# Filling TensorE's first waits with identity products, writing its order by hand, and pulling the next batch's memory and first softmax into that order

## The chip, the cores and the metric

The kernel runs on one core of a Trainium2 chip. The metric is the device time of one execution in microseconds (us). A NeuronCore has a matrix engine (TensorE, PE in the profile, with PEld for its weight loads), a vector engine (VectorE, DVE), a scalar engine (ScalarE, ACT), GpSimd (POOL), and SyncE (SP), which here issues most of the transfers. Each engine runs its own list of instructions in order and waits on semaphores for the others.

## The reference

The program is an attention with a compressed memory, followed by two wide feed-forward layers. All arrays are float32.

```python
# q, k, v: [4, 8, 576, 64]; phi: [4, 8, 576, 32]
a = exp(phi - max(phi, axis=2)); a = a / (sum(a, axis=2) + 1e-09)   # over the sequence
k_m = einsum('bhsm,bhsd->bhmd', a, k); v_m = einsum('bhsm,bhsd->bhmd', a, v)
scores = (1 / sqrt(64)) * q @ k_m.T                                  # 32 memory slots
attn = softmax(scores); x = attn @ v_m                               # [2304, 512] over heads
h = maximum(x @ w_in1, 0); y = (h * h) @ w_out1                      # 512 -> 2048 -> 512
h = y @ w_in2; out = (h * tanh(softplus(h))) @ w_out2                # 512 -> 2048 -> 512
```

The weights reach the kernel as 64-bit floats and are turned into float32 on the chip.

## The kernel before

**Stages.** For each batch, `phi` is exponentiated along the sequence (`kv_soft`, L415 on), transposed on TensorE (`kv_turn`, tiles `pt` and `et`), and multiplied with k and v (`kv_mem`, tile `pk`); `kv_heads` turns the result into `kT` and `vT`. One batch has two halves of 288 tokens. `attn_unit` makes one half's scores (tile `psc`, L511) and runs their softmax in steps: two transposes, a maximum and a subtraction on VectorE (tile `x`), an exponential on ScalarE, then sum, reciprocal and product on VectorE, a transpose back (`at`), and a split into a high part (`ah`, ScalarE) and a low part (`al`, VectorE). v's memory is multiplied into the first weight matrix beforehand (`w_part`, tiles `pw` and `wp`), so that a half's hidden columns are six products of `ah` and `al` with `wp` (`h_products`, L655 to L657). ScalarE takes relu, square and high part (`s`, `g`), VectorE the low part of `g`, and twelve products L622 to L624 add one hidden chunk of 128 columns into four accumulators (`mm2_step`).

**Weights.** A slab of 512 KB of raw words (`raw_i` for w_in1, `raw_o` for w_out1, named i0, i1, o0 and so on below) is loaded by SyncE. ScalarE prepares it with one instruction ("pre"), VectorE joins the words with two ("first", L230, and "second", L236); a slab of w_out1 then gets a high part on ScalarE (`o1h`, L219) and a low part on VectorE (`o1l`, L279).

**What sets the order.** The helper `written(engine)` ties the instructions that are traced inside it to the order of the code, on the engines named. Around `first_memory()` and `first_tile()` it holds for VectorE and ScalarE: all of the first half's work (hidden chunks 0 to 3 of batch 0, half 0), the softmax of half 1, and the weight slabs they need stand in an order written by hand. TensorE's own order there is left to a scheduler, with a table `ahead` that puts four hidden products behind chosen products of the next batch's memory. The next batch's memory and its first softmax are made after that (`lanes = kv_later(1) + attn_later(1, 0)` in the loop over `subs`). TensorE starts with eight products of the identity with itself (`warm`, L714).

**Transfers.** SyncE has eight completion semaphores, so a transfer is issued only after the eighth before it has landed; the first 61 us of loads land one behind the other.

Of the kernel before, what the change touches and what calls it, by code (L numbers as in the profile page):

```python
# [18 lines left out]
P = 128  # L19
# [19 lines left out]
def body(tc, q, kvm, kvt, phi, w_in1, w_out1, w_in2, w_out2, out):  # L39
    nc = tc.nc  # L40
# [37 lines left out]
    def load_phi(b, p):  # L78
        nc.sync.dma_start(phi_t[p][:, at[p]:at[p] + S], phi[b, p])
# [14 lines left out]
    def load_q(b, half):  # L94

        q_t[b, half] = []
        for i in range(2):
            if b < 2 and half == 1:
                t = wo.tile([P, 2, T], F32, tag=f"wo{'hl'[i]}4", name=f"q{b}{half}{i}")
            else:  # L100
                t = Y.tile([P, 2, T], F32, tag="q", name=f"q{b}{half}{i}", bufs=2)
            nc.sync.dma_start(
                t.rearrange("p g t -> p (g t)"), q[b, half, :, 2 * i * T:2 * (i + 1) * T])
            q_t[b, half].append(t)
# [9 lines left out]
    def load_first(i):  # L114
        for p in range(2):
            nc.sync.dma_start(kv_t[0, p][i].rearrange("p g c d -> p (g c d)"), kvm[0, p, i])
        nc.sync.dma_start(tails[:, i].rearrange("p g d -> p (g d)"), kvt[0, i])

    load_first(0)
    load_q(0, 0)  # L120
# [285 lines left out]
    def banks2(name):  # L406
# [2 lines left out]
    rc_t, et_t, kk_t, kT, vT = {}, {}, {}, {}, {}  # L409

    done_pe = {}
    ahead = {(0, 1, 0): ("pt", 1, 0), (0, 1, 1): ("pk", 1, 0), (0, 1, 2): ("pk", 1, 1),
             (0, 1, 3): ("psc", 1, 0)}

    def kv_soft(b, p):  # L415

# [57 lines left out]
    def kv_heads(b, which, tag):  # L474

        ps = bank(tag, f"pkt{b}{which[0]}")
        for i in which:
            done_pe["pkt", b] = nc.tensor.transpose(
                ps[:, i * P:i * P + P], kk_t[b, "k"][:, i].rearrange("p a d -> p (a d)"), ident)
        if 0 in which:  # L480
            kT[b] = Y.tile([P, P], F32, tag="kT", name=f"kT{b}", bufs=2)
            if which == (0,):
                nc.vector.tensor_scalar_mul(kT[b], ps[:, :P], 0.125)
            else:
                nc.scalar.mul(kT[b], ps[:, :P], 0.125)
        if 1 in which:
            vT[b] = Y.tile([P, P], F32, tag="vT", name=f"vT{b}", bufs=2)
            (nc.scalar.copy if which == (1,) else nc.vector.tensor_copy)(vT[b], ps[:, P:2 * P])

    def kv_unit(b, tag, nxt):  # L490
        for p in range(2):
# [214 lines left out]
    c1.hold = True  # L706
    c1.load(1)
    load_first(1)
    c1.load(4)
    load_q(0, 1)  # L710
    c1.load(3)
    warm = bank("acc3", "warm")
    for _ in range(N_WARM):
        nc.tensor.matmul(warm[:, :P], ident, ident, start=True, stop=True)  # L714


    def first_memory():
# [8 lines left out]
    def next_loads():  # L726
        load_phi(1, 0)
        load_phi(1, 1)
        load_kv(1, 0)
        load_tail(1)  # L730
        kv_t[1, 1] = tuple(page([P, 4, NC, D], F32, f"kv11{i}") for i in "kv")
        for i in range(2):
            nc.sync.dma_start(kv_t[1, 1][i].rearrange("p g c d -> p (g c d)"), kvm[1, 1, i])
        c1.load(1)
        load_q(1, 0)

    def first_tile():


        conv = c1.turn  # L740
        at00, at01 = (attn_unit(0, half, nxt, True) for half, nxt in (
            (0, None), (1, lambda: load_q(1, 1))))
        out_of, g, s = [], {}, {}

        def h(fc):
            s[fc] = h_products(0, 0, fc, ("mm", "b0")), X.tile([P, T], F32, tag="s", name=f"s00_{fc}", bufs=3)
            g[fc] = X.tile([P, 2, T], F32R, tag="g", name=f"g00_{fc}", bufs=4)

        def relu(fc):
            marks["step"] = nc.scalar.activation(s[fc][1], s[fc][0], AF.Relu)  # L750

        def square(fc):
            nc.scalar.activation(s[fc][1], s[fc][1], AF.Square)

        def high(fc):
            nc.scalar.copy(g[fc][:, 0], s[fc][1])

        def low(fc):
            marks["lo"] = nc.vector.tensor_sub(g[fc][:, 1], s[fc][1], g[fc][:, 0].bitcast(F32))

        def mm2(fc):
            pend.append((mm2_step, (
                out_of[0], fc, fc == 0, fc == GROUPS[0] - 1, g[fc][:, 0], g[fc][:, 1], out_of[1])))

        next(at00)
        next(at00)
        conv("pre", "i1", 0)
        next(at00)
        conv("first", "i1", 0)
        conv("second", "i1", 0)  # L770
        kv_mem(0, 0, (1,), "acc3")
        kv_mem(0, 1, (1,), "acc0")
        kv_heads(0, (1,), "acc1")
        with written(mybir.EngineType.SP):
            next_loads()
        conv("pre", "i1", 1)
        next(at00)
        next(at00)
        w_low = w_part(0, 0, 0, P, True)
        next(at00)  # L780
        w_low()
        conv("first", "i1", 1)
        conv("pre", "o1", 0)
        next(at00)
        conv("second", "i1", 1)
        out_of += acc_of(0, 0, 0, GROUPS[0])
        h(0)
        conv("first", "o1", 0)
        conv("pre", "i1", 2)
        relu(0)  # L790
        w_low = w_part(0, 0, P, 2 * P, True)
        conv("second", "o1", 0)
        with written(mybir.EngineType.SP):
            c1.load(3)
        conv("high", "o1", 0)
        square(0)
        high(0)
        w_low()
        h(1)
        conv("first", "i1", 2)  # L800
        conv("low", "o1", 0)
        low(0)
        mm2(0)
        run_pend(0)
        conv("pre", "i1", 3)
        conv("second", "i1", 2)
        relu(1)
        square(1)
        conv("first", "i1", 3)
        conv("second", "i1", 3)  # L810
        high(1)
        conv("pre", "o1", 1)
        low(1)
        w_low = w_part(0, 1, 0, 256, True)
        conv("first", "o1", 1)
        conv("second", "o1", 1)
        conv("high", "o1", 1)
        w_low()
        conv("low", "o1", 1)
        next(at01)  # L820
        h(2)
        h(3)
        mm2(1)
        run_pend(0)
        relu(2)
        square(2)
        high(2)
        next(at01)
        relu(3)
        square(3)  # L830
        next(at01)
        low(2)
        mm2(2)
        high(3)
        conv("pre", "o1", 2)
        conv("pre", "o1", 3)
        kv_soft(1, 0)
        next(at01)
        next(at01)
        next(at01)  # L840
        kv_soft(1, 1)
        next(at01)
        conv("first", "o1", 2)
        conv("second", "o1", 2)
        conv("high", "o1", 2)
        low(3)
        mm2(3)
        conv("first", "o1", 3)
        conv("low", "o1", 2)
        conv("second", "o1", 3)  # L850
        marks["step"] = conv("high", "o1", 3)
        conv("low", "o1", 3)

    def lazy(f):
        yield from f()
# [55 lines left out]
    for i, (f0, f1, b, half) in enumerate(subs):  # L911
        final = i == len(subs) - 1
        if i == 0:
# [3 lines left out]
            c1.hold = False  # L917
            c1.store()
            c1.load(2 * GROUPS[0] - 3)
            lanes = kv_later(1) + attn_later(1, 0)  # L920
            run_step(lanes, 7)
            continue
        elif i == 1:
            assert (0, 1) in a_t
# [446 lines left out]
```

## Time and profile before

| | us |
|---|---|
| median of 3 runs (lowest, highest) | 771.23 (769.04, 771.65) |
| the profiled execution | 770.25 |
| its span, first to last instruction | 768.3 |
| PE busy | 735.0 |
| DVE busy | 530.5 |
| ACT busy | 425.4 |

The profiled execution takes 1.95 us more than its span; its own time lies 1.0 us under the median. PE is busy for 96% of the span and idle for 33.3 us. Times in the text count from the span's start.

### The profile page before, as it was taken

How to read it: one execution, taken by the hardware profiler on the slowest of the kernel's cores; microseconds unless marked ns; L12 is line 12 of the kernel's file. 1: busy time of each engine (PE TensorE's matmuls, PEld its weight loads, DVE VectorE, ACT ScalarE, POOL GpSimd, SP SyncE). 2: the span in 40 equal slices, each digit the busy share in tenths (PEclk: the TensorE clock that was granted, in tenths of full speed). 3: DMA queues.
4: the chain of work that ended last, by engine and by line, in shares of the span. 5: the costliest groups of instructions: out<-in, count | busy, mean ns of one | idle time of the engine just before them, and what ended most of it. 6: DMA issues, size and time to landing. Idle time of an engine off the chain costs nothing. (4 is left out here: it accounts for less than half of the span.)

```text
span 768.3 us, 16333 instructions
## 1 busy us (share of the span) xinstructions
PE 735.0 (96%) x5984; PEld 695.9 (91%) x5984; DVE 530.5 (69%) x1068; ACT 425.4 (55%) x964; POOL 131.5 (17%) x176
## 2 busy tenths in 40 slices
PE   5799999999998999999998999999999999999997
PEld 4587898999887889999998999989999989999997
DVE  4779936437678779778889746883846793646583
ACT  3676956656647678766755435642334652434552
POOL 0000000001122223223224301230411050111040
PEclk9799999999999999999999999999999999999999
DMA  9992516117898778678869989788978888778881
GB/s 340 404 409 95 190 37 227 68 30 261 284 341 298 264 267 320 248 276 300 307 240 352 308 263 345 240 257 271 320 270 252 247 250 281 241 251 263 247 267 60
DMA packets 89439, 195.84 MB, mean 255 GB/s; under 512 B 9872, under 2 KB 22672, under 8 KB 89360
## 3 DMA queue, kind: packets, MB, share of 16 engines
q1 hardware_dynamic: 80400, 165.45, 65.1%
q0 software_dynamic: 8960, 29.37, 9.7%
q8 instruction: 47, 0.77, 0.4%
q14 instruction: 32, 0.26, 0.1%
HBM read 151.78 MB, written 42.99 MB: 254 GB/s over the span
## 5 line engine op out<-in xcount | busy, mean ns | idle before, releaser
L622 PE MATMUL a<-g,o1h 128*128 128x288 f32 x512 | 148.7, 300 | 4.1 <-ACT g L680 4.1
L623 PE MATMUL a<-g,o1l 128*128 128x288 f32 x512 | 147.8, 297 | 0.0
L624 PE MATMUL a<-g,o1h 128*128 128x288 f32 x512 | 131.9, 296 | 0.5 <-DVE g L683 0.5
L1225 DVE TENSOR_TENSOR opl<-a,oph 128x384 fp32r<-128x384 f32 x144 | 95.9, 681 | 47.9 <-ACT oph L1224 47.7
L1180 PE MATMUL hb<-ych,u 128*128 128x384 f32 x336 | 113.2, 337 | 3.4 <-DMA u<-wf_i 2.0
L1181 PE MATMUL hb<-ycl,u 128*128 128x384 f32 x336 | 113.0, 336 | 0.0
L1182 PE MATMUL hb<-ych,u 128*128 128x384 f32 x336 | 110.2, 336 | 0.0
L1224 ACT CAST oph<-a 128x384 fp32r<-128x384 f32 x144 | 73.8, 513 | 62.9 <-PE b22acc L1246 7.8
L622 PEld LDWEIGHTS a<-g,o1h 128*128 128x128 f32 x512 | 95.9, 189 | 11.1 <-ACT g L680 6.6
L623 PEld LDWEIGHTS a<-g,o1l 128*128 128x128 f32 x512 | 96.5, 189 | 0.0
L624 PEld LDWEIGHTS a<-g,o1h 128*128 128x128 f32 x512 | 89.9, 189 | 4.5 <-DVE g L683 1.4
L1186 ACT ACTIVATE a<-hs 128x384 f32<-128x384 f32 x72 | 37.6, 525 | 97.9 <-DVE hs L1190 97.9
L675 ACT ACTIVATE s<-h 128x288 f32<-128x288 f32 x124 | 50.9, 412 | 68.9 <-PE h L657 61.7
L655 PE MATMUL h<-ah,wp 128*128 128x288 f32 x256 | 79.7, 313 | 2.9 <-ACT wp L563 1.3
L683 DVE TENSOR_TENSOR g<-s,g 128x288 fp32r<-128x288 f32 x124 | 56.1, 453 | 32.7 <-ACT g L680 31.5
L368 POOL DMA_DIRECT2D wf_i<-st x56 | 30.5, 547 | 278.5 <-DVE st L367 263.6
L656 PE MATMUL h<-al,wp 128*128 128x288 f32 x256 | 76.6, 300 | 0.3 <-DVE al L547 0.3
L657 PE MATMUL h<-ah,wp 128*128 128x288 f32 x256 | 75.8, 297 | 0.0
L1190 DVE TENSOR_TENSOR hs<-hu,hb 128x384 f32<-128x384 f32 x72 | 39.6, 552 | 40.0 <-PE hb L1182 39.6
L1180 PEld LDWEIGHTS hb<-ych,u 128*128 128x128 f32 x336 | 63.1, 188 | 4.0 <-DMA u<-wf_i 2.3
L1181 PEld LDWEIGHTS hb<-ycl,u 128*128 128x128 f32 x336 | 63.0, 188 | 0.0
L1182 PEld LDWEIGHTS hb<-ych,u 128*128 128x128 f32 x336 | 62.9, 188 | 0.0
(265 smaller groups left out, 1748.2 us busy)
## 6 DMA issues: line engine op xcount, KB each, us to landing
u<-wf_i SPq DMA_DIRECT2D x168, 256.0 KB, 3.9
u<-wf_o SPq DMA_DIRECT2D x168, 256.0 KB, 3.3
raw_i<-in_moe_w_in_dram SPq DMA_DIRECT2D x32, 512.0 KB, 4.6
raw_o<-in_moe_w_out_dram SPq DMA_DIRECT2D x32, 512.0 KB, 7.7
wf_i<-st POOLq DMA_DIRECT2D x56, 256.0 KB, 5.0
wf_o<-st POOLq DMA_DIRECT2D x56, 256.0 KB, 4.6
win1r<-w_i SPq DMA_DIRECT2D x17, 512.0 KB, 5.5
kv<-in_kvm_dram SPq DMA_DIRECT2D x5, 1024.0 KB, 9.3
```

Of the source, the lines that this page charges most:

```text
L622: nc.tensor.matmul(o, wh[:, c, cs], sh, start=first, stop=False)
L623: nc.tensor.matmul(o, wl[:, c, cs], sh, start=False, stop=False)
L624: nc.tensor.matmul(o, wh[:, c, cs], sl, start=False, stop=last)
L655: nc.tensor.matmul(ph, w[:, 0, hg, fs], hi[:, hg], start=(hg == 0), stop=False)
L656: nc.tensor.matmul(ph, w[:, 0, hg, fs], lo[:, hg], start=False, stop=False)
L657: nc.tensor.matmul(ph, w[:, 1, hg, fs], hi[:, hg], start=False, stop=(hg == 1))
L683: marks["lo"] = nc.vector.tensor_sub(sl, s, sh.bitcast(F32))
L1180: nc.tensor.matmul(ps, wh, yh[:, d], start=(j < 4 and d == 0), stop=False, **kw)
L1181: nc.tensor.matmul(ps, wh, yl[:, d], start=False, stop=False, **kw)
L1182: nc.tensor.matmul(ps, wl, yh[:, d], start=False, stop=end, **kw)
L1224: marks["hi"] = nc.scalar.copy(hi, x)
L1225: marks["lo"] = sub(lo, x, hi.bitcast(F32))
```

## The change

1. `fill(n, tag)`: n products of the identity with itself into a PSUM bank that is free at that place. There are seven such groups in `first_tile`, of 4, 7, 8, 3, 3, 5 and 5 products.
2. `written(PE)` is opened at the start of `first_tile` and closed after the second half of batch 1's memory. Two entries of `ahead` are left.
3. Batch 1's memory (`kv_soft`, `kv_turn`, `kv_mem`, `kv_heads`) and the first softmax of batch 1 (`at10`) are called inside `first_tile`, hence in the written order of VectorE and ScalarE; the two `lanes` that did this before are gone.
4. The first softmax's `ah` stands ahead of the `wp` cast on ScalarE, and `al` ahead of the low part on VectorE.
5. Loads: the short tails of k and v come one place earlier; slab o1 comes ahead of batch 1's `phi`, and the queries of half 1 behind it, with slabs o2 and o3 spread between batch 1's loads.
6. `vT` of batch 1 is copied by ScalarE, no longer by VectorE.

```diff
-        nc.sync.dma_start(tails[:, i].rearrange("p g d -> p (g d)"), kvt[0, i])
+            if p == 0:
+                nc.sync.dma_start(tails[:, i].rearrange("p g d -> p (g d)"), kvt[0, i])
...
-    ahead = {(0, 1, 0): ("pt", 1, 0), (0, 1, 1): ("pk", 1, 0), (0, 1, 2): ("pk", 1, 1),
-             (0, 1, 3): ("psc", 1, 0)}
+    ahead = {(0, 1, 0): ("pk", 1, 1), (0, 1, 1): ("psc", 1, 0)}
...
-            (nc.scalar.copy if which == (1,) else nc.vector.tensor_copy)(vT[b], ps[:, P:2 * P])
+            (nc.scalar.copy if b < 2 else nc.vector.tensor_copy)(vT[b], ps[:, P:2 * P])
...
-    c1.load(4)
-    load_q(0, 1)
-    c1.load(3)
+    c1.load(5)
...
+    def fill(n, tag):
+        ps = bank(tag, "fill")
+        for _ in range(n):
+            nc.tensor.matmul(ps[:, :P], ident, ident, start=True, stop=True)
...
         load_phi(1, 1)
+        load_q(0, 1)
+        c1.load(1)
         load_kv(1, 0)
...
+        pe = written(mybir.EngineType.PE)
+        pe.__enter__()
         next(at00)
+        fill(4, "mm")
         next(at00)
...
         kv_mem(0, 0, (1,), "acc3")
+        fill(7, "mm")
         kv_mem(0, 1, (1,), "acc0")
...
+        next(at01, None)
+        fill(5, "mm")
+        kv_mem(1, 1, (0, 1), "b0")
+        pe.__exit__(None, None, None)
+        conv("second", "o1", 2)
+        conv("high", "o1", 2)
+        kv_heads(1, (0, 1), "b0")
         low(2)
         mm2(2)
-        high(3)
-        conv("pre", "o1", 2)
         conv("pre", "o1", 3)
...
+        conv("low", "o1", 2)
+        conv("first", "o1", 3)
+        next(at10)
+        next(at10)
+        next(at10)
+        conv("second", "o1", 3)
+        marks["step"] = conv("high", "o1", 3)
         low(3)
         mm2(3)
...
+        next(at10)
         conv("low", "o1", 3)
+        next(at10)
+        next(at10)
+        next(at10, None)
+        load_phi(2, 0)
+        load_phi(2, 1)
+        load_kv(2, 0)
+        load_tail(2)
...
-            lanes = kv_later(1) + attn_later(1, 0)
-            run_step(lanes, 7)
```

Names below read so: `psc00` are the scores of batch 0, half 0; `pk001` the product of the first pair of heads with v; `h01_3` hidden chunk 3 of batch 0, half 1; `g00_3` the squared chunk 3 of half 0. TensorE from the first scores to the first hidden product, before:

```order
L511 MATMUL psc00_218<-q001_94,kT0_216 32x288 x4
L463 MATMUL pk001_238<-kv00_85,et00_147 32x64 x16
L463 MATMUL pk011_260<-kv01v_87,et01_159 32x64 x7
L463 MATMUL pk001_238<-kt0_88,et00_147 32x64 x4
L463 MATMUL pk011_260<-kv01v_87,et01_159 32x64 x9
L463 MATMUL pk011_260<-kt0_88,et01_159 32x64 x4
L478 MATMUL pkt01_282<-ident_96,kk0_190 128x128
L557 MATMUL pw000_310<-win1_0_235,vT0_284 32x128 x8
L655 MATMUL h00_0_333<-ah00_321,wp00_319 128x288
```

and now:

```order
L511 MATMUL psc00_210<-q001_94,kT0_208 32x288 x4
L717 MATMUL fill_219<-ident_96 128x128 x4
L463 MATMUL pk001_235<-kv00_85,et00_139 32x64 x16
L463 MATMUL pk001_235<-kt0_88,et00_139 32x64 x4
L717 MATMUL fill_257<-ident_96 128x128 x7
L463 MATMUL pk011_265<-kv01v_87,et01_151 32x64 x16
L463 MATMUL pk011_265<-kt0_88,et01_151 32x64 x4
L478 MATMUL pkt01_287<-ident_96,kk0_182 128x128
L557 MATMUL pw000_327<-win1_0_232,vT0_289 32x128 x8
L717 MATMUL fill_338<-ident_96 128x128 x8
L655 MATMUL h00_0_353<-ah00_324,wp00_336 128x288
```

Nineteen identity products now stand between the first scores and the first hidden product.

VectorE around the low part of slab o3 (`o1l1<-ct_o1_3`), which the last products of hidden chunk 3 need, before:

```order
L471 TENSOR_SCALAR kk1_554<-pk100_533,rc10_481 128x2x64
L279 TENSOR_TENSOR o1l1_502<-ct_o1_2_498,o1h1_501 128x512
L236 SCALAR_TENSOR_TENSOR ct_o1_3_505<-raw_o1_3_126,ct_o1_3_505 128x512
L279 TENSOR_TENSOR o1l1_502<-ct_o1_3_505,o1h1_501 128x512
L236 SCALAR_TENSOR_TENSOR win1_2_670<-raw_i1_4_296,win1_2_670 128x4x128
L683 TENSOR_TENSOR g01_0_654<-s01_0_653,g01_0_654 128x288
```

and now, where `x10` and `ssm10` belong to the first softmax of batch 1:

```order
L530 TENSOR_REDUCE ssm10_664<-x10_654 128x18
L237 SCALAR_TENSOR_TENSOR win1_2_718<-raw_i1_4_313,win1_2_718 128x4x128
L237 SCALAR_TENSOR_TENSOR ct_o1_4_797<-raw_o1_4_403,ct_o1_4_797 128x512
L564 TENSOR_TENSOR wp10_787<-pw100_778,wp10_787 128x512
L531 TENSOR_SCALAR ssm10_664<-ssm10_664 128x18
L683 TENSOR_TENSOR g01_2_757<-s01_2_756,g01_2_757 128x288
L532 RECIPROCAL ssm10_664<-ssm10_664 128x18
L533 TENSOR_TENSOR x10_654<-x10_654,ssm10_664 128x576
L280 TENSOR_TENSOR o1l1_627<-ct_o1_3_639,o1h1_626 128x512
L536 STREAM_TRANSPOSE at10_670<-x10_654 128x576
```

It stood behind the first memory product of batch 1; it now stands behind that batch's first normalised softmax.

TensorE at the products that need it, before:

```order
L657 MATMUL h01_1_662<-ah01_490,wp00_319 128x288
L622 MATMUL a0000_329<-g00_3_450,o1h1_501 128x288
L623 MATMUL a0000_329<-g00_3_450,o1l1_502 128x288
L624 MATMUL a0000_329<-g00_3_450,o1h1_501 128x288
L622 MATMUL a0001_330<-g00_3_450,o1h1_501 128x288
L623 MATMUL a0001_330<-g00_3_450,o1l1_502 128x288
```

and now:

```order
L622 MATMUL a0003_352<-g00_3_491,o1h1_626 128x288
L655 MATMUL h01_3_790<-ah01_573,wp01_440 128x288
L656 MATMUL h01_3_790<-al01_574,wp01_440 128x288
L657 MATMUL h01_3_790<-ah01_573,wp01_440 128x288
...
L557 MATMUL pw110_820<-win1_1_398,vT1_634 32x256 x8
L623 MATMUL a0000_349<-g00_3_491,o1l1_627 128x288
L624 MATMUL a0000_349<-g00_3_491,o1h1_626 128x288
```

Hidden chunks 2 and 3 of half 1 and batch 1's two weight products (`pw100`, `pw110`) moved ahead of the eight products L623 and L624 of `g00_3`; the second products of half 1 (accumulators `a0100` on) moved behind them.

## Rows read from the trace of the kernel before

**Rows 1.** Windows: length; busy PE, PEld, DVE, ACT, POOL; clock; DMA share, GB/s.

```profile
15.37:29.02 13.65, 10.94 (x116) 7.75 (x107) 10.43 (x21) 8.11 (x18) 0.00 (x0) 0.50 1.03 402
29.02:39.26 10.24, 5.36 (x57) 4.26 (x61) 8.09 (x16) 6.95 (x15) 0.00 (x0) 1.00 1.03 408
39.26:42.68 3.42, 3.42 (x46) 3.04 (x36) 3.17 (x10) 1.60 (x4) 0.00 (x0) 0.50 1.04 423
61.80:200.00 138.20, 137.30 (x1178) 124.76 (x1171) 84.78 (x186) 90.58 (x216) 3.40 (x6) 1.00 0.41 138
```

**Rows 2.** PE's waits in 0 to 62 us: total, times, longest.

```profile
PE pt L439 <- ACT phi L422: 3.4, 1, 3.4
PE psc L511 <- DVE wp L564: 1.9, 1, 1.9
PE pk L463 <- DMA kv01v<-in_kvm_dram: 1.6, 1, 1.6
PE pk L463 <- DMA kv<-in_kvm_dram: 1.4, 2, 1.2
PE pk L463 <- DMA kt<-in_kvt_dram: 1.2, 1, 1.2
PE h L655 <- ACT ah L544: 1.1, 1, 1.1
```

**Rows 3.** PE's timeline: start, length, instruction, count, idle before it.

```profile
1.53 3.75 PE L714 MATMUL warm<-ident 128*128 128x128 f32 x16 [1.53 <-POOL ident masks.py:199]
...
24.87 1.17 PE L622 MATMUL a<-g,o1h 128*128 128x288 f32 x4
...
38.96 1.71 PE L463 MATMUL pk<-kv,et 128*32 128x128 f32 x32 [0.78 <-ACT et L442]
...
43.24 0.69 PE L622 MATMUL a<-g,o1h 128*128 128x288 f32 x4
...
47.06 0.29 PE L622 MATMUL a<-g,o1h 128*128 128x288 f32 x1
47.19 0.29 PE L623 MATMUL a<-g,o1l 128*128 128x288 f32 x1
...
56.27 0.66 PE L557 MATMUL pw<-win,vT 64*32 64x256 f32 x16
...
61.15 0.72 PE L511 MATMUL psc<-q,kT 64*32 64x288 f32 x16 [1.85 <-DVE wp L564]
61.80 0.53 PE L655 MATMUL h<-ah,wp 128*128 128x288 f32 x2
```

**Rows 4.** Windows as in rows 1: to the end of `al10`, and its last part.

```profile
59.02:62.02 3.00, 1.15 (x33) 0.40 (x18) 2.84 (x7) 1.29 (x3) 0.00 (x0) 1.00 0.22 82
20.00:62.02 42.02, 34.44 (x389) 28.12 (x389) 32.41 (x68) 27.10 (x60) 0.00 (x0) 0.85 0.97 382
```

**Rows 5.** DVE's timeline, columns as in rows 3.

```profile
19.75 0.75 DVE L547 TENSOR_TENSOR al<-at,ah 128x576 fp32r<-128x576 f32 x1
...
27.05 0.42 DVE L230 TENSOR_SCALAR ct_o<-raw_o 128x512 int32<-128x512 int32 x1
27.58 0.69 DVE L236 SCALAR_TENSOR_TENSOR ct_o<-raw_o,ct_o 128x512 int32<-128x512 int32 x1
...
50.84 0.28 DVE L488 COPY vT<-pkt 128x128 f32<-128x128 f32 x1
...
56.05 0.46 DVE L683 TENSOR_TENSOR g<-s,g 128x288 fp32r<-128x288 f32 x1 [0.25 <-ACT g L680]
```

**Rows 6.** ACT's timeline, columns as in rows 3.

```profile
29.09 0.59 ACT L563 CAST wp<-pw 128x512 fp32r<-128x512 f32 x1 [2.04 <-PE pw L557]
29.58 0.62 ACT L219 CAST o1h<-ct_o 128x512 fp32r<-128x512 f32 x1
...
44.45 0.69 ACT L200 ACTIVATE raw_i<-raw_i 128x512 f32<-128x512 f32 x1
45.03 0.39 ACT L675 ACTIVATE s<-h 128x288 f32<-128x288 f32 x1
```

More of the change, by code (lines that the diff above doesn't have):

```diff
@@ L735, in next_loads @@
         load_q(1, 0)
+        c1.load(1)
     def first_tile():
         conv = c1.turn
[L741 to L742 removed]
+        at00 = attn_unit(0, 0, None, True)
+        at01 = attn_unit(0, 1, lambda: load_q(1, 1), True)
+        at10 = attn_unit(1, 0, lambda: load_q(2, 0), True)
         out_of, g, s = [], {}, {}
@@ L778, in first_tile @@
         next(at00)
+        conv("first", "i1", 1)
+        next(at00)
         w_low = w_part(0, 0, 0, P, True)
-        next(at00)
+        fill(8, "mm")
+        next(at00, None)
         w_low()
[L782 to L785, printed above, removed]
         out_of += acc_of(0, 0, 0, GROUPS[0])
         h(0)
+        conv("pre", "o1", 0)
+        conv("second", "i1", 1)
+        conv("pre", "i1", 2)
         conv("first", "o1", 0)
-        conv("pre", "i1", 2)
         relu(0)
+        conv("second", "o1", 0)
         w_low = w_part(0, 0, P, 2 * P, True)
-        conv("second", "o1", 0)
+        square(0)
+        w_low()
+        fill(3, "b0")
+        h(1)
+        conv("high", "o1", 0)
+        high(0)
+        conv("first", "i1", 2)
+        conv("low", "o1", 0)
         with written(mybir.EngineType.SP):
             c1.load(3)
[L795 to L801, printed above, removed]
+        relu(1)
         low(0)
+        fill(3, "mm")
         mm2(0)
@@ L806, in first_tile @@
         conv("second", "i1", 2)
-        relu(1)
         square(1)
+        high(1)
         conv("first", "i1", 3)
         conv("second", "i1", 3)
-        high(1)
+        w_low = w_part(0, 1, 0, 256, True)
         conv("pre", "o1", 1)
         low(1)
-        w_low = w_part(0, 1, 0, 256, True)
         conv("first", "o1", 1)
         conv("second", "o1", 1)
+        w_low()
         conv("high", "o1", 1)
-        w_low()
+        conv("pre", "o1", 2)
+        kv_soft(1, 0)
+        fill(5, "b0")
+        next(at01)
         conv("low", "o1", 1)
-        next(at01)
         h(2)
         h(3)
+        next(at01)
+        relu(2)
+        relu(3)
+        kv_turn(1, 0)
         mm2(1)
         run_pend(0)
-        relu(2)
+        next(at01)
+        kv_soft(1, 1)
         square(2)
         high(2)
-        next(at01)
-        relu(3)
         square(3)
         next(at01)
+        kv_mem(1, 0, (0, 1), "b0")
+        kv_turn(1, 1)
+        high(3)
+        next(at01)
+        conv("first", "o1", 2)
+        next(at01)
+        next(at01, None)
[5 more added lines that the diff above has]
+        kv_heads(1, (0, 1), "b0")
         low(2)
         mm2(2)
-        high(3)
-        conv("pre", "o1", 2)
         conv("pre", "o1", 3)
[L837 to L845, printed above, removed]
+        conv("low", "o1", 2)
[5 more added lines that the diff above has]
+        marks["step"] = conv("high", "o1", 3)
         low(3)
         mm2(3)
[L848 to L851, printed above, removed]
+        next(at10)
         conv("low", "o1", 3)
+        next(at10)
[5 more added lines that the diff above has]
+        load_tail(2)
     def lazy(f):
```

## Prediction

> **What bounds the kernel now.** I read the windows of the whole span first, then TensorE's waits and its timeline over the first 62 us, then VectorE's and ScalarE's timelines there. From 61.80 us to 200 us TensorE is busy for 137.30 of 138.20 us [rows 1], and from some 180 us on every engine's order is the same in both programs, so the change is worth what it does to the time at which that full stretch begins. The reader is to see two losses ahead of it. One is idle time: TensorE waits 3.4 us for an exponential of batch 1's `phi`, 1.9 us ahead of the last scores, and for loads of k and v at the start [rows 2]. The other is the clock: it is granted at 0.50, the lower of its two levels (1.2 GHz), from 15.37 to 29.02 us and again from 39.26 to 42.68 us, and at 1.00 (2.4 GHz) between and after [rows 1]. Four products of 288 columns take 1.17 us at the lower level and 0.69 us at the higher one [rows 3]. The fall at 39.26 comes after the 3.4 us wait and another of 0.78 us [rows 2, 3].
>
> **The common point.** I compare both programs where TensorE starts the first hidden product of batch 1 with all products of batch 0's first two tiles done. Before, this is at 61.80 us [rows 3].
>
> **What the identity products cost.** There are 35. Before, eight take 3.75 us, 0.47 each [rows 3]; scaled by the two levels of the 288-column products (0.69 over 1.17) this is 0.28, and 0.24 if the level halves it. I take 0.25, and keep 0.24 and 0.47 as the ends. The Trainium skill (FP8 and Floating Point Precision, TensorE Precision Notes) says that a true float32 product makes four passes through the array; four passes of 128 columns at 2.4 GHz would be an estimate of 0.21 us each, by which the 35 cost 7.5 us instead of 8.8. At 0.25 the first four (1.0 us) lie in the wait for v of the first heads (1.2 us), the seven (1.75 us) in that for v of the second heads (1.6 us), and the eight (2.0 us) between the first weight product and the moment when `wp`'s low part is ready; the waits they cover are in rows 2. The others lie in waits that the new order itself makes. So I cost them at nothing, and what the first groups return is the clock: I take 1.00 from 15.37 us on. If that cover is gone they cost 0.22 us more each, which is a rival below.
>
> **What the start gains.** At the higher level the weight product ahead of the eight ends near 17.8 us by my count, the eight at 19.8 and the first hidden chunk, six products at 0.13, near 20.6 us. It would then be VectorE and ScalarE that set the pace, since they have the same work per weight slab. The shifted tails of k and v put a transfer of a quarter of a slab ahead of another; the bytes in front of the second memory product stay the same, so the 1.2 us wait for the tail [rows 2] only changes its name, and I count 0.1 us. The reordered slabs and queries land one behind the other as before, a few slab times ahead of their use: nothing. The copy of `vT` on ScalarE takes 0.28 us from VectorE [rows 5] and is counted below.
>
> **VectorE's sum to the last part of slab o3.** In the new order the low part of o3 (`o1l1<-ct_o1_3`) stands behind batch 1's whole first softmax but its transposes back. TensorE's eight products L623 and L624 of `g00_3` need it, and behind them in its queue are all second products of the second tile, for they reuse the same accumulators. So this one instruction decides. VectorE's work up to it, from the trace: from 20.00 us to the end of `al10` it is busy 32.41 us [rows 4]. Off come the last six operations, which now stand behind it or, for the evacuation copies, later still: 2.84 us as a group [rows 4]; the low part of `g01_3`, 0.46; `vT`, 0.28 [rows 5]. Off comes also what is done by 20.00 us already: `al` of the first tile runs at 19.75 for 0.75 us before [rows 5], and now comes ahead of `wp`'s low part and near 18.7 us, so 0.5 us of it and, as an estimate, 0.3 us of the next joining. 32.41 - 2.84 - 0.46 - 0.28 - 0.8 = 28.0 us.
>
> To this come the waits that the written order makes on VectorE:
> - The second joining of o1 waits for ScalarE's preparation, which stands behind the `wp01` cast, which waits for TensorE's weight product: 0.66 + 0.59 + 0.69 [rows 3, 6] and three handovers of 0.05, 2.1 us in all, while VectorE has a low part and a first joining, 0.46 + 0.42 [rows 5]: 1.2 us.
> - `al` of the second tile waits for `ah`, a cast that I count like `o1h`'s: 0.62 [rows 6] and three handovers against one first joining, 0.42: 0.35 us.
> - The low part of o2 waits for `o1h`, behind relu of `h01_0` and one preparation: five hidden products of 0.13, 0.39 + 0.69 + 0.62 [rows 3, 6] and handovers, 2.5 us, against 0.28 + 0.69 + 0.46 of its own [rows 5] (the scaling of the memory is counted like the copy of `vT`): 1.05 us.
> - The low part of `g01_0` waits behind ScalarE's `kT`, `vT`, a preparation, square and cast (2 x 0.28 + 0.69 + 2 x 0.39 [rows 5, 6]), 2.0 us against 0.69 + 0.42: 0.9 us.
> - Smaller ones and handovers, an estimate: 0.5 us.
>
> Together 4.0 us, and the low part of o3 ends at 20.0 + 28.0 + 4.0 = 52.0 us.
>
> **TensorE behind it.** It then owes 8 products of `g00_3`, 48 of the second tile and the last scores: 56 at 0.13 us (the spacing of L622 and L623) and 0.65 us from 61.15 to 61.80 [rows 3], 8.0 us. I see nothing there that is late: the accumulators are copied by ScalarE as the eight products go, and `ah10`, `al10` follow within 3 us. The common point comes at 60.0 to 60.1 us instead of 61.80: **1.7 us earlier**. TensorE's own waits do not disappear: worked along the new order, it stands idle about 1.3 us ahead of `psc01`, 1.4 us ahead of the first products of `g00_2`, and 1.8, 0.8, 0.8 and 1.4 us in the stretch from 45 to 52 us. The 3.4 us wait and the lower clock go, and these take their place, since VectorE is then nearly full.
>
> **Against its own time.** 770.25 - 1.7 = 768.55 us for an execution like the profiled one, which lies 1.0 us under the median of the three runs. For the median, 771.23 - 1.7 = 769.5 us.
>
> **The rivals.**
> - *VectorE waits less than I summed.* Its work alone would end the low part at 48.0 us; each wait that proves hidden is worth its whole length. Half of them gone gives 3.7 us, all gone 5.7 us: 765.5 to 767.5 us. For it speaks that ScalarE has room (27.10 busy of 42.02 us [rows 4]); against it, that its instructions stand in a written order too, so the casts cannot come sooner than what is ahead of them.
> - *The clock falls in the new waits.* Between 45 and 52 us TensorE would be idle for over half the time. In 29.02 to 39.26 us it was busy for 5.36 of 10.24 us and the clock fell at the end [rows 1]. The lower level would then hold for the first few us of the owed products; a full stretch of 3.42 us at that level [rows 1] loses half, 1.7 us: no change, 771.2 us. The Trainium skill (TensorE: Matmul & The Clock Gate, A second HAM failure mode) says that short idle spells between groups of products, repeated often enough, make the clock swing between its levels; by that rule this rival holds. The trace agrees for one place, the fall at 39.26, and disagrees for another: several waits of up to 1.2 us lie ahead of 15.37 us at the clock 1.00.
> - *The identity products run at the lower level: slower.* If the clock falls at 15.37 us all the same, the eight and the following three cost 0.22 us more each, 2.4 us; the first hidden chunk runs at 0.24 instead of 0.13 a product, 0.65 us; and the memory and weight products ahead about 0.5 us. They stand ahead of the hidden products in a queue that cannot pass them. 3.6 us later from there on, less the 1.7 us: 1.9 us slower, 773.1 us. It decides where the granted clock is 0.50 when the eight begin. For it speaks that the clock did fall there; against it, that the waits of 1.2 and 1.6 us ahead of that point are what the first eleven products fill.
>
> **How the numbers follow.** About 0.3%, 2.3 us, is what can be told from no change here. My forecast has 0.50; VectorE waiting less 0.25; the clock in the new waits 0.13; the lower level at the start 0.12. The forecast's own range is 768.0 to 771.2 us, a fifth of it beyond 2.3 us faster: 0.10. The first rival adds 0.24, which makes 0.35 for faster with rounding. Slower by over 2.3 us is two fifths of the last rival and a part for stalls in the full stretch that I do not see, 0.11; the rest, 0.54, is no change that can be told. The range reaches to all of VectorE's waits gone and to the last rival: 765.6 to 773.0 us.
>
> **What would show it.** Right: the clock at 1.00 throughout 15.4 to 29 us; `psc01` near 28.5 us instead of 31; the low part of o3 on VectorE ending near 52 us with L623 of `g00_3` starting at once; batch 1's first hidden products among the second tile's, and the owed work done near 60 us; windows behind 200 us unchanged. Wrong: L623 of `g00_3` starting without a wait before 50 us (the first rival), 0.50 after 49 us (the second) or at the eight products (the third), or TensorE idle for more than 1 us between 62 and 180 us, which no step here foresees.

## The result, and the profile after

The changed kernel takes 774.59 us (774.05 to 777.44, six runs), the kernel before 770.88 us in the same comparison (769.04 to 771.65): a ratio of 1.0058, 95% interval 1.0038 to 1.0077. It is slower by 3.7 us; forecast was 1.7 us faster, and 774.6 lies outside the range of 765.6 to 773.0 us. A second measurement (e9 below) gives 1.0048, 1.0027 to 1.0068. Among the experiments, two runs of e11 (797.9 and 1427.1 us) are disturbed and left out of its ratio, and so is its profile, which is of the longer one. The profiled execution after takes 774.65 us, its span is 772.5 us (768.3 before).

Windows after, columns as in [rows 1]; the fourth and fifth are new:

```profile
15.37:29.02 13.65, 11.35 (x155) 9.23 (x154) 11.22 (x24) 8.63 (x19) 0.00 (x0) 1.00 1.04 403
29.02:39.26 10.24, 10.05 (x186) 8.86 (x187) 9.33 (x22) 7.34 (x16) 0.00 (x0) 1.00 1.03 405
39.26:42.68 3.42, 2.09 (x26) 1.23 (x25) 1.59 (x5) 3.12 (x8) 0.00 (x0) 1.00 1.03 413
50.73:57.55 6.82, 5.86 (x40) 4.55 (x47) 6.11 (x14) 3.88 (x10) 0.00 (x0) 0.50 1.04 404
422.78:429.60 6.82, 5.86 (x18) 5.86 (x19) 5.96 (x13) 2.24 (x5) 3.70 (x5) 0.50 0.78 276
61.80:200.00 138.20, 137.17 (x1141) 123.18 (x1144) 81.82 (x178) 89.53 (x213) 3.39 (x6) 1.00 0.39 130
```

The reader is to see that the two stretches of [rows 1] at 0.50 are gone, as forecast, and that two others have come, at 50.73 and at 422.78 us. Behind 61.80 us TensorE is as full as before (137.17 against 137.30 of 138.20 us), and yet time is lost there too: it gets through 1141 instructions instead of 1178.

TensorE's waits in 0 to 62 us after, in the columns of [rows 2]:

```profile
PE a L622 <- ACT o1h L220: 2.8, 2, 1.5
PE psc L511 <- DVE wp L564: 1.3, 1, 1.3
PE a L623 <- DVE o1l L280: 0.9, 1, 0.9
PE pw L557 <- DVE wp L564: 0.8, 1, 0.8
PE h L655 <- ACT s L675: 0.6, 1, 0.6
```

The 3.4 us wait for the exponential and the 1.9 us wait ahead of the last scores have gone; the waits in their place were foreseen within 0.5 us each. TensorE's timeline around the place that the prediction called decisive, columns as in [rows 3]:

```profile
17.99 2.05 PE L717 MATMUL fill<-ident 128*128 128x128 f32 x16
...
47.56 0.79 PE L622 MATMUL a<-g,o1h 128*128 128x288 f32 x4 [1.49 <-ACT o1h L220]
48.91 0.40 PE L655 MATMUL h<-ah,wp 128*128 128x288 f32 x1 [0.57 <-ACT s L675]
...
50.78 1.11 PE L557 MATMUL pw<-win,vT 64*32 64x256 f32 x16 [0.81 <-DVE wp L564]
52.80 0.61 PE L623 MATMUL a<-g,o1l 128*128 128x288 f32 x1 [0.90 <-DVE o1l L280]
53.20 0.44 PE L624 MATMUL a<-g,o1h 128*128 128x288 f32 x1
53.44 0.44 PE L623 MATMUL a<-g,o1l 128*128 128x288 f32 x1
...
57.17 0.86 PE L511 MATMUL psc<-q,kT 64*32 64x288 f32 x14
...
61.90 0.29 PE L657 MATMUL h<-ah,wp 128*128 128x288 f32 x1
62.12 0.67 PE L511 MATMUL psc<-q,kT 64*32 64x288 f32 x2
...
62.96 0.30 PE L623 MATMUL a<-g,o1l 128*128 128x288 f32 x1
```

Three things stand here. L623 starts at 52.80 us. The 17 products from there to 57.17 us take 4.37 us, 0.24 us apart, where [rows 3] have 0.13: the lower clock. In e1 below the same 17, behind like waits, run at 1.00 and take 56.42 - 53.98 = 2.44 us:

```profile
53.98 0.40 PE L625 MATMUL a<-g,o1l 128*128 128x288 f32 x1 [1.34 <-DVE o1l L280]
...
56.42 0.72 PE L512 MATMUL psc<-q,kT 64*32 64x288 f32 x16
```

And the scores psc11 stand in two pieces (14 and 2 records, two for each float32 product), with 288-column products between. From 61.90 to 62.96 us a single score product costs 1.06 us where two spacings of 0.13 us would be: 0.80 us.

VectorE's row that decides L623, columns as in [rows 5], and the window from 20 us to its end, as in [rows 1]:

```profile
52.06 0.68 DVE L280 TENSOR_TENSOR o1l<-ct_o,o1h 128x512 fp32r<-128x512 f32 x1
20.00:52.74 32.74, 26.01 (x349) 20.49 (x348) 28.07 (x61) 23.87 (x52) 0.00 (x0) 0.97 1.04 403
```

**Where the 3.4 us come from up to 135 us.** Chunk 9 of batch 1, half 0, is the first place behind which TensorE has done the same work in both programs; it begins at 131.96 us before and 135.35 us after; this start is the "mark" below. A piece is a run of narrow products (pw or psc, up to eight of one group) with no 288-column product between them. From the scores psc11 to the mark there are 13 pieces before and 16 after. A piece costs about 0.75 us, however few of the eight products are in it. TensorE after:

```profile
90.22 0.29 PE L657 MATMUL h<-ah,wp 128*128 128x288 f32 x1
90.44 0.62 PE L557 MATMUL pw<-win,vT 64*32 64x256 f32 x2
...
91.23 0.30 PE L623 MATMUL a<-g,o1l 128*128 128x288 f32 x1
...
93.35 0.29 PE L657 MATMUL h<-ah,wp 128*128 128x288 f32 x1
93.58 0.64 PE L557 MATMUL pw<-win,vT 64*32 64x256 f32 x8
...
94.38 0.30 PE L656 MATMUL h<-al,wp 128*128 128x288 f32 x1
```

One product: 91.23 - 90.22 - 0.26 = 0.75 us. Four products: 94.38 - 93.35 - 0.26 = 0.77 us. Before, pw120 stands in two pieces; after, in four. The sum: -1.7 forecast, +0.75 for the late L623 (52.80 instead of the 52.0 forecast and a handover of 0.05), +1.9 for the clock (4.37 against 2.44), +2.3 for three more pieces, which is +3.25 against the measured +3.4. From there to 395 us the difference shrinks to 1.2 us (TensorE's waits behind 200 us are shorter after). Then, between 419 and 430 us, it grows from 1.1 to 4.5 us with the lower clock from 422.78 us, and it is 4.3 us at the end. So the second fall weighs as much in the end as the whole difference at the mark.

### The profile page after: what moved, and what is told of

Same layout as the page of the kernel before. It is cut to its first block, busy times and chain, and to the rows that moved or that the text cites. A ratio compares the mean times of both kernels' runs of the same rounds, so it can differ in the third digit from the quotient of the medians.

```text
span 772.5 us, 16478 instructions
## 1 busy us (share of the span) xinstructions
PE 745.1 (96%) x6054; PEld 704.8 (91%) x6054; DVE 529.3 (69%) x1067; ACT 425.6 (55%) x965; POOL 132.5 (17%) x176
## 4 chain that ended last, share of the span: by engine, by line
PE 74%; issue 10%; DVE 7%; DMA 3%; POOL 3%; ACT 3%; SPq 1%; POOLq 0%; DVEq 0%; ACTq 0%
PE hb L1211 7%; PE hb L1212 7%; PE hb L1213 7%; PE a L622 6%; PE a L623 6%; PE a L624 6%; PE h L655 3%; POOL wf_o L369 3%; PE h L656 3%; PE h L657 3%; PE pw L557 2%; PE pk L463 1%; DMA kv<-in_kvm_dram 1%; DVE opl L1256 1%; PE fill L717 1%
## 5 line engine op out<-in xcount | busy, mean ns | idle before, releaser
L622 PE MATMUL a<-g,o1h 128*128 128x288 f32 x512 | 149.4, 300 | 5.4 <-ACT o1h L220 2.8
L623 PE MATMUL a<-g,o1l 128*128 128x288 f32 x512 | 149.6, 298 | 0.9 <-DVE o1l L280 0.9
L624 PE MATMUL a<-g,o1h 128*128 128x288 f32 x512 | 135.6, 297 | 0.0
L1211 PE MATMUL hb<-ych,u 128*128 128x384 f32 x336 | 114.4, 341 | 3.8 <-DVE hu L1232 2.1
L1213 PE MATMUL hb<-ych,u 128*128 128x384 f32 x336 | 111.3, 339 | 0.0
L622 PEld LDWEIGHTS a<-g,o1h 128*128 128x128 f32 x512 | 95.9, 188 | 12.7 <-ACT g L680 5.0
L623 PEld LDWEIGHTS a<-g,o1l 128*128 128x128 f32 x512 | 97.2, 190 | 1.8 <-DVE o1l L280 1.8
L624 PEld LDWEIGHTS a<-g,o1h 128*128 128x128 f32 x512 | 91.8, 190 | 3.4 <-issue 1.7
L1211 PEld LDWEIGHTS hb<-ych,u 128*128 128x128 f32 x336 | 64.0, 191 | 4.7 <-DVE hu L1232 2.5
L1213 PEld LDWEIGHTS hb<-ych,u 128*128 128x128 f32 x336 | 63.7, 190 | 0.0
```

Of the source, the lines that this page charges most:

```text
L622: nc.tensor.matmul(o, wh[:, c, cs], sh, start=first, stop=False)
L623: nc.tensor.matmul(o, wl[:, c, cs], sh, start=False, stop=False)
L624: nc.tensor.matmul(o, wh[:, c, cs], sl, start=False, stop=last)
L1211: nc.tensor.matmul(ps, wh, yh[:, d], start=(j < 4 and d == 0), stop=False, **kw)
L1213: nc.tensor.matmul(ps, wl, yh[:, d], start=False, stop=end, **kw)
```

## The experiments

All of them carry the rule of e1, but e9. With that rule two more groups of weight products stand ahead of the mark, so marks with it compare among themselves.

| | median us | ratio to before, 95% interval | mark, us |
|---|---|---|---|
| e1 after, whole pieces | 764.66 | 0.9928 (0.9906 to 0.9951) | 128.8 |
| e2 before, whole pieces | 765.74 | 0.9930 (0.9912 to 0.9947) | 130.7 |
| e3 e1 + 12 identity products | 763.09 | 0.9901 (0.9883 to 0.9918) | 127.9 |
| e4 e1 + low part early | 763.13 | 0.9912 (0.9891 to 0.9933) | 128.8 |
| e5 e1 without identity products | 768.44 | 0.9970 (0.9955 to 0.9984) | 134.9 |
| e6 e3 + last four pieces whole | 764.96 | 0.9929 (0.9913 to 0.9944) | 129.9 |
| e7 e6 + 16 narrow products | 766.57 | 0.9946 (0.9928 to 0.9965) | 129.0 |
| e8 e6 + 16 full products | 764.48 | 0.9924 (0.9905 to 0.9943) | 128.2 |
| e9 after again | 774.38 | 1.0048 (1.0027 to 1.0068) | 135.0 |
| e10 e3 + e4 | 761.37 | 0.9888 (0.9868 to 0.9907) | 127.4 |
| e11 e6, subtractions on VectorE | 760.35 | 0.9873 (0.9851 to 0.9895) | - |
| e12 e10 + e11 | 758.54 | 0.9852 (0.9827 to 0.9877) | 126.8 |

**e1 and e2: do the pieces cost what they seem to?** The first part of the edit is in `w_part`, the second in `attn_unit`; the scheduler then sets each group as a whole.

```diff
+        with tc.high_priority() if (b, j) != (0, 0) and b < 2 else contextlib.nullcontext():
             for g in range(4):
                 for p in range(2):
                     nc.tensor.matmul(ps[...], vT[b][...], wt["i1", j][...], start=True, stop=True)
...
+        with tc.high_priority() if (b, half) == (1, 1) else contextlib.nullcontext():
             for g in range(4):
                 for p in range(2):
                     done_pe["psc", b, half] = nc.tensor.matmul(...)
```

> The changed kernel with one rule added: the products of batches 0 and 1 with the first weights (pw) and the scores psc11 get a higher priority in the order, so that each group of eight stands in one piece. Theory: every piece of narrow products among the 288-column products costs about 0.75 us, whatever its length (after: 0.74 us for a piece of one product, 0.79 for eight). The changed kernel has 51 such pieces, this one 41, the kernel before 48: ten pieces fewer give 7.5 us, so about 767 us, and TensorE's first 150 entries, up to the scores psc11, are the same, so the clock is 0.50 from about 50.7 to 57.5 us as in the changed kernel. Rival: the pieces stand in waits of TensorE and cost nothing; then 774.5 us, and the three extra pieces explain nothing of the loss.

> The kernel before with the same rule: 41 pieces instead of 48. Theory: seven pieces at 0.75 us, 5.2 us, so about 765.5 us; against the changed kernel with the rule it is then 1.5 us faster, which is what is left of the loss of 3.7 us without the three extra pieces (2.2 us): the clock and the late low part against the gain at the start. Rival: the pieces cost nothing: 770.5 us, and the difference to the changed kernel with the rule stays 3.7 us.

Measured: 1.30 points of ratio less than the changed kernel (7.5 us expected, about 10 measured) and 0.70 points less than the kernel before (5.2 expected, 5.4 measured). With whole pieces both programs take the same within their intervals, where 1.5 us in favour of e2 was expected: what was left of the change was no loss. For e1's further 2.5 us the clock is a likely cause: its profile has neither the fall at 50.73 us nor that at 422.78 us, but one at 11.47 us. It is not shown: over all runs the mean clock is only 0.002 higher than in the changed kernel (0.9935 against 0.9915). Windows of e1:

```profile
11.47:14.89 3.42, 3.42 (x44) 2.30 (x38) 2.29 (x5) 0.66 (x1) 0.00 (x0) 0.50 1.04 412
50.73:57.55 6.82, 4.68 (x56) 3.33 (x55) 6.42 (x14) 4.75 (x12) 0.00 (x0) 1.00 1.04 402
```

TensorE's first 150 entries are the same as in the changed kernel, and the waits ahead of L623 are no shorter (1.48, 0.57, 0.80 and 1.34 us), so my expectation on that point was wrong: this order does not fix where the clock falls. L623 comes at 53.98 us, 1.2 us later than in the changed kernel, and psc11 2.4 us behind it instead of 4.4.

**e3: do the waits from 45.8 to 52.8 us lower the clock?** The first part of the edit is in `a_tile`, the second in `w_part` behind its eight products.

```diff
             ph = h_products(b, half, fc, banks)
+            if (b, half) == (0, 1) and fc in {2: 5, 3: 4}:
+                with tc.issue_after(done_pe["h", b, half, fc].ins):
+                    fill({2: 5, 3: 4}[fc], "b0")
...
+        if (b, j) == (1, 1):
+            with tc.issue_after(last.ins):
+                fill(3, "b0")
```

> The first of these kernels with twelve further identity products, in TensorE's waits of the changed kernel between 45.8 and 52.8 us: five ahead of the first products of hidden chunk 3 of half 0, four behind hidden chunk 3 of half 1, three behind batch 1's second weight product. Theory: the clock falls at 50.7 us because of these waits; with them filled it stays at 1.00, the 16 products from 52.8 us take 2.1 instead of 4.4 us, and the kernel is 2.3 us faster than the first one, 764.7 us. Rival: the waits are VectorE's, the next low part is late all the same, and the higher clock only makes TensorE wait longer behind: less than 0.5 us.

TensorE in e3 (L629 and L630 are L623 and L624 there):

```profile
45.54 1.28 PE L727 MATMUL fill<-ident 128*128 128x128 f32 x10
...
52.42 0.40 PE L629 MATMUL a<-g,o1l 128*128 128x288 f32 x1 [0.48 <-DVE o1l L281]
52.66 0.29 PE L630 MATMUL a<-g,o1h 128*128 128x288 f32 x1
52.79 0.30 PE L629 MATMUL a<-g,o1l 128*128 128x288 f32 x1
```

The mean granted clock of its four runs is 0.998 to 1.000 (e1: 0.988 to 0.998, the changed kernel: 0.988 to 0.996), and the products behind L623 are 0.13 us apart. It is the runs' clocks that tell e3 from e1, not this place: e1's profile does not fall here either. The time is 1.6 us less than e1's; the intervals of the two overlap, so the higher clock is shown and what it is worth only likely.

**e4: does the low part of o3 decide?**

```diff
         next(at10)
         next(at10)
-        next(at10)
         conv("second", "o1", 3)
         marks["step"] = conv("high", "o1", 3)
+        next(at10)
         low(3)
         mm2(3)
-        next(at10)
         conv("low", "o1", 3)
         next(at10)
+        next(at10)
```

> The first of these kernels with VectorE's second joining of slab o3 one step of batch 1's softmax earlier, and the low part of o3 ahead of that softmax's sum, reciprocal and product instead of behind them. Theory: the low part decides when L623 of hidden chunk 3 starts; four operations of 0.75, 0.17, 0.27 and 0.76 us now stand behind it, so it ends about 1.7 us earlier, near 51 us, and the kernel gains up to 1.7 us, 765.4 us, more if the shorter wait holds the clock. Rival: TensorE then waits as much for the split of batch 1's softmax at its first hidden product, and nothing is gained.

L623 starts at 48.98 us, 3.4 us earlier than in e3, whose clock is 1.00 as here, and yet the mark is at 128.8 us against 127.9. It starts 5.0 us earlier than in e1, whose mark is 128.8 us too. So that instruction alone does not decide. One of TensorE's waits in 100 to 130 us of e4, and VectorE's timeline there:

```profile
PE a L624 <- DVE ys L639: 1.5, 1, 1.5
```
```profile
119.23 0.43 DVE L231 TENSOR_SCALAR win<-raw_i 128x512 int32<-128x512 int32 x1 [1.11 <-DMA raw_i<-in_moe_w_in_dram]
119.57 0.81 DVE L639 TENSOR_TENSOR ys<-a,ys 128x288 f32<-128x288 f32 x2
```

VectorE's joining stands ahead of the accumulators' sums (ys) and waits for a weight slab; TensorE waits 1.5 us for the sums. Part of what comes early is taken back there by a transfer. In e10, which has the early low part too, TensorE does not wait there, and its mark is only 0.5 us ahead of e3's; where the rest goes was not found. The time (763.13) is also a mixture: two runs of the six have a clock of 0.992 and take 765.8 and 766.2 us, the other four 0.998 or more and 761.9 to 763.7. These 3.3 us between runs of one kernel are the plainest sign here of what the lower clock costs.

**e5: what are the first 35 identity products worth?** `for _ in range(n)` in `fill` becomes `range(0)`.

> The changed kernel with whole pieces (the first kernel of the series) and none of its 35 identity products. Theory of the prediction: they hold the clock at 1.00 from 15.4 to 29 us, and without them the stretch runs at 0.50 as before, psc01 comes about 1 us later and the kernel is 1 to 2 us slower, 766 us. Rival: VectorE and ScalarE set the pace from 20 us on, so neither the products nor the clock at the start count: within 0.5 us of 764.7. Second rival: in TensorE's queue they push the first hidden products back (20.2 us against 19.7 in the kernel before), and without them it is 0.5 to 1 us faster.

```profile
12.55:29.62 17.07, 12.29 (x153) 8.90 (x153) 12.54 (x25) 7.95 (x19) 0.00 (x0) 0.50 1.03 402
53.51:60.34 6.83, 4.46 (x42) 2.39 (x41) 6.02 (x12) 4.03 (x10) 0.00 (x0) 0.50 0.94 347
```

By the medians 3.8 us slower than e1, by the ratios 3.2: twice what was expected, and both rivals fall. The clock is 0.979 to 0.987 in its twelve runs. The part of the prediction on the identity products holds.

**e6 to e8: the last pieces, and the price of one by itself.** e6 puts the rule of e1 on psc30 and `w_pair` too. e7 and e8 add one product behind each hidden chunk of batch 2, half 1, with the first of these two lines in e7 and the second in e8:

```diff
+        if (b, half) == (2, 1):
+            with tc.high_priority(), tc.issue_after(done_pe["h", b, half, fc].ins):
+                nc.tensor.matmul(bk[:M, T:T + D], ident[:M, :M], ident[:M, :D], start=True, stop=True)
+                nc.tensor.matmul(bk[:, T:T + P], ident, ident, start=True, stop=True)
```

> The kernel with whole pieces and the twelve further identity products, with the last four extra pieces taken out too: the scores psc30 and the weight products of batch 3 (pw30p) stand in one piece each, 37 pieces instead of 41. Theory: four times 0.75 us, 3 us, so 760.1 us. Rival: at that place (about 300 us) TensorE waits for something else anyway: 763 us.

> The kernel just before with 16 useless products of 32 rows by 64 columns, one behind each hidden chunk of batch 2, half 1, written into unused columns of that chunk's bank. They add 14 pieces. Theory: a piece costs about 0.75 us whatever is in it, less the two intervals of 0.13 us that are there anyway, so about 0.6 us are added by each: 8.5 to 10.5 us slower than without them, about 770 us. Rival: what costs is the work in the pieces (eight products with 256 columns), and a product of 64 columns costs under 0.1 us: under 1.6 us slower.

> The same with 16 useless products of 128 rows by 128 columns instead (the identity with itself, float32). If the price of a piece comes from the narrow shape (32 rows), each costs only its own 0.25 us as in the waits at the start: about 4 us slower than without them, 764 us. If it comes from float32 among products of the other type, it costs as much as a narrow piece or more: 9 to 12 us slower, 769 to 772 us.

TensorE in e7, then in e8, at one such product:

```profile
286.83 0.29 PE L665 MATMUL h<-ah,wp 128*128 128x288 f32 x1
287.06 0.29 PE L669 MATMUL h<-ident 32*32 32x64 f32 x2
...
287.52 0.30 PE L630 MATMUL a<-g,o1l 128*128 128x288 f32 x1
```
```profile
286.37 0.30 PE L665 MATMUL h<-ah,wp 128*128 128x288 f32 x1
286.50 0.38 PE L669 MATMUL h<-ident 128*128 128x128 f32 x2
...
286.86 0.29 PE L630 MATMUL a<-g,o1l 128*128 128x288 f32 x1
```

The narrow product of 64 columns costs 287.52 - 286.83 - 0.26 = 0.43 us, the full one 0.23 us, its own length. So neither side was right for e7. With 0.75 us at 256 columns, 192 columns make 0.32 us; by that, as an estimate, 64 make 0.11, and 0.32 us are the fixed price of a piece (an estimate across two shapes: pw has 64 rows, this product 32). "Whatever is in it" holds for the number of products, not for their width. Half 1 of batch 2, from its second hidden chunk to batch 3's first, takes 39.5 us in e6, 45.2 in e7 and 42.5 in e8: +5.7 and +3.0 for the 15 products in it, 0.38 and 0.20 us each. The whole time does not show it (+1.6 and -0.5), because e6 lost later what it had gained: up to batch 3 it is 2.6 us ahead of e3, and then the second layer's first units take it back. So e6's expectation (760.1 us) and its rival (763) were both missed. TensorE's wait there, then VectorE's and GpSimd's timelines and a window, all of e6:

```profile
PE hb L1222 <- DVE hu L1243: 5.4, 1, 5.4
```
```profile
408.24 4.58 DVE L369 TENSOR_TENSOR st<-raw_o,st 128x256 fp32r<-128x256 f32 x2
```
```profile
408.63 1.81 POOL L1120 TENSOR_TENSOR yt<-yr,yt 128x768 f32<-128x768 f32 x1
410.39 1.80 POOL L1123 TENSOR_TENSOR yr<-yr,yr 128x768 f32<-128x768 f32 x1
```
```profile
410.87:417.70 6.83, 3.90 (x12) 3.90 (x13) 6.37 (x11) 1.05 (x2) 3.92 (x5) 0.50 0.75 270
```

One of the two subtractions takes 4.24 us of the 4.58. But every profile with GpSimd's subtractions, that of the kernel before too, has one VectorE instruction of 3.8 to 5.0 us near there. In e3 it is another one:

```profile
411.60 4.52 DVE L392 TENSOR_TENSOR ct_o<-raw_o,ct_o 128x256 f32<-128x256 f32 x1
```

TensorE then waits for VectorE for 0.9 us, and the clock stays at 1.00. The 210 hidden products of the passage (hb020 to hb070, from 405.12 us in e3 and 402.82 in e6) take 40.4 us in e3 and 44.1 in e6. Over all profiles that passage goes with the clock: 40.3 to 41.0 us without a fall, 42.0 with 3.4 us at the lower level (e9, e10), 43.2 and 44.1 with 6.8 us (the changed kernel, e6).

**e9: the changed kernel again.** Its expectation, and the two windows in which its profile has the lower clock:

> The changed kernel once more, unaltered, for a second profile. Theory: the order of its pieces is the same, so the first hidden product of chunk 9 of batch 1 (h10_9) comes 3 to 4 us later than in the kernel before, whose 132.0 us is the mark, by the pieces (2.2 us), the low part (0.7) and the clock; but where the clock is 0.50 is not fixed by the order: in a second profile the stretches from 50.7 and from 422.8 us may lie elsewhere or be gone, and the passage from 411 to 455 us, which took 2.9 us longer than before in the first profile, then takes 40.5 us as before. Rival: both stretches belong to the order and come again within 2 us of the same places.

```profile
49.85:56.67 6.82, 5.13 (x34) 4.10 (x33) 6.11 (x14) 4.61 (x11) 0.00 (x0) 0.50 1.04 399
425.31:428.73 3.42, 3.42 (x12) 3.42 (x11) 3.42 (x7) 2.02 (x5) 0.93 (x1) 0.50 0.88 317
```

The mark is 3.0 us later than before, and both falls come again within 2.6 us, the second for half as long. The rival was nearer: in both profiles of this program they come.

**e10 to e12: towards a faster kernel.** e10 joins e4 to e3, with seven identity products where its order waits; e11 is e6 with this edit; e12 has all of it.

```diff
-        sub = nc.vector.tensor_sub if i == 0 else nc.gpsimd.tensor_sub
+        sub = nc.vector.tensor_sub
```

> Whole pieces, the low part of o3 ahead of batch 1's softmax steps, and seven further identity products in the waits that this order has (three ahead of the first products of hidden chunk 3, four behind hidden chunk 3 of half 1). Theory: the early low part alone was worth nothing beyond the clock (763.1 us with either), since VectorE then holds up TensorE at 118 us behind a weight slab; so 763 us again, with the clock at 0.998 or more. Rival: the two add up, 761.5 us.

> The kernel with all pieces whole and the twelve further identity products, and GpSimd's three subtractions of 128 rows by 768 columns per tile of the second layer given to VectorE. Theory: at 408 to 413 us VectorE's subtractions of 128 by 256 took 4.6 us instead of 0.4 to 0.8 because GpSimd's subtractions ran beside them; TensorE waited 5.4 us and the clock fell, so what the last four pieces gave (4.4 us up to 305 us) was lost there. Without GpSimd's subtractions the passage from 401 to 446 us takes 40.5 instead of 45.2 us, and the kernel 760 us. Rival: the wait is for slabs or stores there (the transfers' share is over 1.0), and it stays: 764 to 765 us.

> All parts that gave something in one kernel: the changed kernel with every piece whole (37), the low part of o3 early, seven further identity products in the waits from 46 to 49 us, and GpSimd's three subtractions per tile of the second layer on VectorE. Theory: the low part and the fills give 1.5 to 3 us against the changed kernel with whole pieces (761.4 us), the last four pieces 3 to 4.4 us up to 305 us, and the passage from hb020 to hb070 (401 to 446 us where GpSimd subtracts beside VectorE) takes 40.5 us and keeps them: 758 us. Rival: the passage is bound by the transfers and stores, takes back what comes early, and the kernel stays at 761 us; then VectorE's long subtractions are still there in the profile.

e10's 761.4 us is the rival's number: early low part and held clock add up, though the intervals with e3 overlap. e11's expectation was met in time (759.2 to 761.9 us, 760 expected). e12 takes 758.54 us, 11.5 us less than the kernel before and 16 less than the changed one. Its profile shows VectorE without GpSimd's work beside it:

```profile
403.85 0.42 DVE L369 TENSOR_TENSOR st<-raw_o,st 128x256 fp32r<-128x256 f32 x1
404.19 0.95 DVE L1122 TENSOR_TENSOR yt<-yr,yr 128x768 f32<-128x768 f32 x1
405.06 0.41 DVE L369 TENSOR_TENSOR st<-raw_o,st 128x256 fp32r<-128x256 f32 x1
```

The long subtractions are gone, TensorE's waits there are 3.1 us in two parts for weight units (u) instead of 5.4 us at once for VectorE, and the clock is 1.00 from 400 to 430 us. The passage that took 44.1 us in e6 takes 40.4. (The 45.2 us of the expectations for e6 fits six products more.)

## Why the prediction was wrong

The step that failed, and that no rival covered, is the one on which the rest stood: "from some 180 us on every engine's order is the same in both programs, so the change is worth what it does to the time at which that full stretch begins". It takes the stretch from 62 to 180 us, where the orders differ, for equal time. It is not: the scheduler, which orders TensorE there, cuts the narrow products (batch 0's and 1's weights and the scores psc11) into 16 pieces instead of 13, at 0.75 us each: 2.3 us up to the mark. The difference was in front of me in the order, and [rows 3] have its price: pw at 56.27 stands for 0.66 us, and psc at 61.15 for 0.65. With whole pieces (e1 against e2) the loss of 3.7 us is gone: 0.9928 against 0.9930. Three more pieces at their own price explain 2.3 us of that; that the rest is the clock is likely, but not shown.

- **The clock at the start**: right. It is 1.00 from 15.37 to 42.68 us, the eight products take 2.05 us (2.0 forecast), and without the 35 products the kernel is 3.2 to 3.8 us slower (e5). That is more than my forecast's whole gain, since without them the clock also falls at 33 and 53 us.
- **VectorE's sum**: 52.74 us for the end of the low part of o3, 52.0 forecast. It was no luck: from 20 us to there VectorE is busy for 28.07 us (28.0 forecast) and waits for 4.7 (4.0 forecast).
- **"This one instruction decides"**: half right. The products behind it did wait 0.9 us, but an L623 that comes 3.4 us earlier gave nothing at the mark (e4 against e3): in e4 a VectorE wait for a later slab is behind it.
- **The clock in the new waits**, the second rival, with a chance of 0.13: it came, and its price was 1.9 us instead of 1.7. It was given too small a chance. What spoke against it, short waits near the start at the clock 1.00, was misread: right behind them, the last of 1.6 us [rows 2], the clock falls at 15.37 us [rows 1]. But such waits do not settle it: from 45.70 to 52.80 us TensorE is busy for 3.33 of 7.10 us and the clock falls at 50.73; in e1, from 46.90 to 54.00 us, it is busy for 2.91 of 7.10 in waits no shorter and the clock stays at 1.00. The Trainium skill (TensorE: Matmul & The Clock Gate, A second HAM failure mode) says that frequent short idle spells make the clock swing; e3 agrees, by 12 identity products in these spells and a clock of 0.998 or more. With the clock and the late low part the sum would be 1.0 us slower, inside the range; the pieces and the second fall took it outside.
- **The identity products at the lower level**, the slower rival: it did not come in the changed kernel, and did once with the same order, at 11.47 us in e1.
- **"Windows behind 200 us unchanged"**: wrong. Equal order is not equal time there: VectorE, GpSimd and the transfers reach the second layer at other times relative to TensorE, the passage near 414 to 457 us took 43.2 us instead of 40.3, with a second fall of the clock in it, 3.4 us of the loss at the end. What sets off that fall was not tested. Why TensorE recovers 2 us between 135 and 395 us after was seen (shorter waits) and not tested.

## What to carry to other kernels

When a part of the order is left to a scheduler, compare the order of the bounding engine past the edited place and price what is cut apart there: here four narrow products in one piece cost 0.77 us and one alone 0.75. Keeping them together gave 5.4 us on the kernel before. Filling TensorE's waits paid here by the clock behind them, not by the waits. It has to cover the waits that the new order makes, too: with those from 46 to 53 us left open the clock fell there in both profiles of the changed kernel.

## What the runs showed of the hardware

- A 128x256 subtraction on VectorE, 0.42 us elsewhere, took 4.24 us while GpSimd made two subtractions of 128x768 one behind the other (e6: 408.24 to 412.48 us, GpSimd 408.63 to 412.19 us); with GpSimd's work on VectorE it is 0.42 and 0.41 us (e12). It isn't always VectorE that is held up: in e3 two such subtractions took 0.76 us together from 408.33 us, inside a GpSimd subtraction of 2.77 us, where the next two took 1.84 and 1.85. The Trainium skill (SBUF — State Buffer, SBUF: two separate sides) says that the two share a pair of ports under an exclusive lock when VectorE has two inputs in SBUF and GpSimd reads SBUF. These rows agree that one is held up for the other's whole instruction; what decides which of the two they do not show.
- Where the clock falls is not fixed by the order: 50.73 and 49.85 us in two profiles of the changed kernel, 11.47 us with the same first 150 entries (e1), and four of e4's six runs have a mean clock of 0.998 or more, two 0.992. The Trainium skill (TensorE: Matmul & The Clock Gate, What's actually happening) says that the number of products at the lower clock when a kernel starts varies from run to run with the phase at the start. For falls, these runs show the like.
- Among 288-column products a narrow one costs 0.43 us with 32 rows and 64 columns (e7) and 0.75 us with 64 rows and 256 columns, and four of the latter in one piece 0.77 us; a full 128x128 float32 one costs 0.23 us (e8).
